# Attention and two MLP layers on one core: second layer in 512-token blocks, float32 scores for three more pairs, q and k in natural order, a new plan

## Chip, core and metric

One Trainium2 chip, one NeuronCore of it. The metric is the device time of one execution in microseconds (us), lower is better. The engines are TensorE (PE: matmuls; PEld: its weight loads), VectorE (DVE), ScalarE (ACT), GpSimd (POOL) and SyncE (SP, which issues most DMAs); SBUF is the on-chip memory, psum the one that matmuls write.

## What is computed

Attention with a threshold, then two MLP layers over the same 2304 = 4 x 576 tokens; everything at float32 accuracy.

```python
def _attn_ref(q, k, v, tau):                       # (4, 8, 576, 64)
    scores = scale * np.matmul(q, k.transpose(0, 1, 3, 2))
    thresh = np.max(scores, axis=-1, keepdims=True) - tau
    scores = np.where(scores >= thresh, scores, -1000000000.0)
    scores = scores - np.max(scores, axis=-1, keepdims=True)
    attn = np.exp(scores)
    attn = attn / (np.sum(attn, axis=-1, keepdims=True) + 1e-09)
    return np.matmul(attn, v)
# x = heads side by side: (2304, 512)
def _moe_ref(x, w_in, w_out):                      # 512 -> 2048 -> 512
    r = np.maximum(x @ w_in, 0.0)
    return (r * r) @ w_out
def _moe2_ref(x, w_in, w_out):
    h = x @ w_in
    sp = np.where(h > 20.0, h, np.log1p(np.exp(np.minimum(h, 20.0))))
    return (h * np.tanh(sp)) @ w_out
```

The four weight matrices come as float64.

## The kernel before

**How the order arises.** The functions of the kernel do not issue instructions. They record operations in a `Plan` (class at line 79): `op({"V": 0.6, "P": 1.24}, fn, r=, w=, x=, due=)` names the engines that may run it (T TensorE, V VectorE, A ScalarE, P GpSimd) with an assumed duration on each, what it reads and writes, and when it is due. `forwards` (line 197) and `backwards` (157) then simulate the engines and choose for each operation an engine and a place, under the assumed durations, the due times and the constants of `PAR` and `BIAS`; it also has a rule for the port that VectorE and GpSimd use together. The program is written out in that order under a manual schedule. So every change of a duration, a due time or a choice can move instructions anywhere.

**Attention.** A pair is two heads of one batch; there are 4 batches of 4 pairs, and a unit is one tile of 128 queries of a pair. `attention` (1005) gives each pair a kind. Kind "d" (batch 0) goes through `job_direct` (678): q and k are loaded in float32 with the two heads as blocks of the free dimension (runs of 1 KB in the memory), and TensorE turns each by 20 small matmuls with the identity; scores are one float32 pass. Kind "s" (batches 1 to 3) goes through `job` (644): q, k, v are loaded in natural order (runs of 256 bytes), scaled by a power of two found from the sums of squares (`pow2`, 551), split into two float16 halves (`split`, 588, lines 600 and 604), turned by DMA, and scores take three float16 passes. In both, `unit` (746) runs the scores, the row maximum (VectorE, line 783, from psum), exp (ScalarE, 806) and the mask with its sum (VectorE, 817, from two SBUF operands). `head` (826) splits the result e into float16 halves (841, and the subtraction at 846 in a piece of 512 and one of 64 columns, on VectorE or GpSimd) where the values are multiplied in float16; batch 0 turns e on TensorE (`values_direct`, 866, line 889).

**Weights.** `weights` (424) fetches one sixteenth of a matrix, [128, 512] float64 as pairs of int32, and rebuilds float32 from the halves by a series of operations on ScalarE (`size`, `rest`), VectorE (`clamp` at 465, `shift` at 477, `sign` at 483; or `factor` on ScalarE and `times`), and to a rounded high part and a low part (`to_hi`, 507; `to_lo`, 519, subtraction at 521). A matmul with weights runs three passes: high-high, high-low, low-high.

```python
            op({"V": 0.34, "P": 1.45}, clamp, x=[w], due=due - 3 + O_CV, two=True)
            op({"V": 0.6}, shift, r=[raw], x=[w], due=due - 2 + O_CV, two=True)
```

**Layers.** Layer one (`first`, 1108, `first_part`, 1116) runs 9 blocks of 256 tokens, each in 8 parts j: two operations of 12 matmuls of 256 columns (`mlp_in`, 1043), ReLU and square, two "down" operations of 12 into the sum `acc`. The first blocks run between units of attention, as soon as batch 0 is done, and the last after it. Layer two (`second`, 1170) runs 9 blocks of 256 tokens in 4 quarters: four `mlp_in` operations into two of three psum places, s0, s1 and the pair (h, o0) (`quarter`, 1028), then softplus and tanh as ScalarE activations (recorded by `act`, 1173, executed at 1179) with steps on VectorE (1223, 1235, gate at 1249), the split into high and low part (511, 521), and four down operations of 6 matmuls of 512 columns:

```python
                for f in range(4):
                    mlp_in(1, 2 * qd + f // 2, f % 2, ph[f // 2], 256 * (f % 2), x, d + 0.1 * f)
```

Of the kernel before, what the change touches and what calls it, by code (L numbers as in the profile page):

```python
# [29 lines left out]
    on=dict(),  # L30
    won=("S", "S"),
    land=1.8,
    lag=1.045,
    turns=("h", "s1"),
    kv=(("nat0", "V1"), ("f1", "nat1"), ("KT1", "f0"), ("V0", "KT0")),
    cd=(-103.359, 8.066, -43.099),
    urg=-3.138,
    rawt=19.607,
    kinds="dddd",
    cgen=0.081,  # L40
    split=(),
    ex=dict(cw=1, cr=22, raw=4, pd=2, sc=4),
    exo=("pd", "cw", "sc", "raw", "cr"),
    blk=list((22.378, 87.527, 172.036, 247.705, 353.772, 474.186, 575.438, 769.06, 852.156)),
    tb2=207.373,
    down2=-110.768,
    sp=(1, 0),
    off=(115.794, 85.638, 120.96, -226.354, 75.139, 25.769, -102.917, -5.246),
    ahead=(13.309, 135.862, 0.835, -119.128, 12.338, 42.57, 40.034, 91.863, 160.78, 84.376),
    start=-49.931,  # L50
    area=dict(sc=("x0", "x1"), hl=("x2",)),
    jobahead=19.218,
    fbi=8,
    stay=-23.036,
    kinds2="ssss",
)
# [22 lines left out]
class Plan:  # L79
# [117 lines left out]
    def forwards(self, succ):  # L197
# [6 lines left out]
        port = 0.0  # L204
# [15 lines left out]
        while count < len(ops):  # L220
# [57 lines left out]
            if o.load is None and (e == "P" or e == "V" and o.two):  # L278
                dur += (0.15 if e == "P" else 0.6) * max(0.0, port - t)
                port = max(port, t + dur)  # L280
# [25 lines left out]
def attention_moe_moe_kernel(ctx: ExitStack, tc: tile.TileContext, q, k, v, tau, w1i, w1o, w2i, w2o, out):  # L306
# [26 lines left out]
    }  # L333
    area = sb.tile([128, 3968], I32, name="area", tag="area")

    def sbuf(place, shape, dt):
        if place in AREA:
            z, n, over = AREA[place]
            n = min(n, math.prod(shape[1:]) * (2 if dt == F16 else 4) // 4)

            def make():
                t = area[:, z:z + n].bitcast(dt)
# [20 lines left out]
    def rot(*places):  # L363
# [7 lines left out]
        "n4": (dict(S=2.95, P=2.75), 1.86, 0.8, 1.9),  # L371
        "q1": (dict(S=0.75, P=0.8), 0.0, 0.4, 0.4), "q2": (dict(S=1.45, P=1.4), 0.62, 0.19, 0.65),
        "w": (dict(S=0.6, P=0.75, A=0.45), 0.0, 1.8, 1.75), "n3": (dict(S=2.3, P=2.0), 1.24, 0.9, 1.6),
        "n2": (dict(S=1.45, P=1.35), 0.62, 0.5, 1.4),
        "xs": (dict(S=0.72, P=0.65), 0.0, 0.36, 0.36), "tail": (dict(S=1.3, P=1.3), 0.6, 0.19, 0.38),
# [46 lines left out]
    W = {}  # L422

    def weights(layer, kind, j, due, places, wplaces):
# [5 lines left out]
        for half in range(2):  # L430
# [15 lines left out]
            def part(t, half=half):  # L446
                if kind == 0:
                    return t()[:, 2 * half:2 * half + 2, :].rearrange("p c f -> p (c f)")
                return t()[:, half, :]
# [929 lines left out]
```

## Time and profile before

| | before |
|---|---|
| time, median of 3 runs | 1058.34 us (1056.44 to 1058.71) |
| the profiled execution | 1057.58 us |
| its span, first to last instruction | 1055.8 us |
| mean granted TensorE clock | 0.987 |
| PE busy | 1012.6 us (96%) |
| DVE busy | 742.9 us (70%) |
| ACT busy | 786.8 us (75%) |
| POOL busy | 119.6 us (11%) |
| first matmul of layer one | 139.8 us after the span's start |
| first matmul of layer two | 685.6 us |
| last matmul | 1050.9 us |

Busy shares are means over stages with different limits, so they are read by stage: attention and weight conversion alone (to 139.8 us), attention with layer one between its units (to about 660), layer two (from 685.6). L392 is the helper `mm` that issues most matmuls; its tile names (acc, h, s, small) say which operation a matmul belongs to.

### The profile page before, as it was taken

The numbers are of one execution on the slowest core, as the hardware profiler recorded it, in microseconds if no ns is written. First come the engines' busy times: TensorE is split into PE (matmuls) and PEld (weight loads), VectorE is DVE, ScalarE is ACT, GpSimd is POOL, SyncE is SP. The second block draws the span as 40 slices with busy tenths as digits, with TensorE's granted clock in tenths as the row PEclk, the third lists the DMA queues.
The fourth block names the chain that finished last, engine by engine and source line by source line (L and its number), as shares of the span: only waits on it lengthen the run. The fifth ranks groups of instructions, "written<-read, shape, count | busy, mean of one in ns | idle before, by whom it ended". The sixth has DMA issues, their size and how long they took to land. (4 is left out here: it accounts for less than half of the span.)

```text
span 1055.8 us, 24074 instructions
## 1 busy us (share of the span) xinstructions
PE 1012.6 (96%) x9484; PEld 915.7 (87%) x9484; DVE 742.9 (70%) x1675; ACT 786.8 (75%) x1301; POOL 119.6 (11%) x132
## 2 busy tenths in 40 slices
PE   6998789799999999999999999899999999999998
PEld 4665478688989898998999999899999999999997
DVE  5999899999888998897574149875454444464443
ACT  5989789787776877776685369978777676596774
POOL 1451333310111111121000000000000000000000
PEclk9999889999999999999999999999999999999999
DMA  9532479889989888976863014410100000000000
GB/s 301 149 125 65 121 160 207 168 155 173 174 153 170 155 185 160 173 156 116 188 212 122 31 37 165 140 55 27 36 14 32 20 21 21 31 30 1 20 21 20
DMA packets 240146, 113.78 MB, mean 108 GB/s; under 512 B 202784, under 2 KB 221728, under 8 KB 240032
## 3 DMA queue, kind: packets, MB, share of 16 engines
q1 hardware_dynamic: 239744, 111.71, 45.9%
q8 instruction: 74, 1.21, 0.5%
q10 hardware_dynamic: 288, 0.52, 0.1%
q14 instruction: 40, 0.33, 0.1%
HBM read 58.33 MB, written 14.16 MB: 69 GB/s over the span
## 5 line engine op out<-in xcount | busy, mean ns | idle before, releaser
L392 PE MATMUL s<-KT,area 64*128 64x64 f16 (+6 forms) x880 | 87.6, 323 | 6.0 <-DVE wi7l L783 1.9
L1175 ACT ACT_TABLE_LOAD x70 | 89.8, 1283 | 1.2
L521 DVE TENSOR_TENSOR gl<-r,gh 128x512 fp32r<-128x512 f32 x83 | 57.0, 687 | 47.1 <-ACT gh L511 45.4
L511 ACT ACTIVATE gh<-r 128x512 fp32r<-128x512 f32 x90 | 56.4, 626 | 31.0 <-PE acc L392 29.0
L806 ACT ACTIVATE e<-area,m 128x576 f32<-128x576 f32 x91 | 68.2, 768 | 15.0 <-DVE hl L846 5.4
L817 DVE SCALAR_TENSOR_TENSOR e<-area,n,e 128x576 f32<-128x576 f32 x91 | 72.6, 814 | 8.0 <-ACT e L806 7.4
L783 DVE TENSOR_SCALAR_CACHE_REDUCE area<-s,c 128x576 f32<-128x576 f32 x91 | 72.1, 812 | 7.3 <-PE s L392 6.7
L1127 ACT ACTIVATE r<-h 128x512 f32<-128x512 f32 x72 | 42.6, 592 | 35.6 <-PE h L392 31.0
L1223 DVE TENSOR_SCALAR area<-area 128x512 f32<-128x512 f32 x37 | 15.7, 426 | 76.0 <-ACT area L1179 75.9
L392 PE MATMUL small<-V,pt 128*128 128x64 f16 (+1 forms) x1680 | 66.4, 196 | 1.7 <-ACT xt L975 0.8
L392 PEld LDWEIGHTS <-pt 128*128 128x128 f16 (+1 forms) x1680 | 56.7, 102 | 10.9 <-issue 7.1
L846 DVE TENSOR_TENSOR hl<-e,hl 128x512 f16<-128x512 f32 (+1 forms) x101 | 61.6, 617 | 4.3 <-ACT hl L841 4.3
L841 ACT ACTIVATE hl<-e 128x576 f16<-128x576 f32 x77 | 51.5, 676 | 13.3 <-DVE e L817 6.0
L846 POOL TENSOR_TENSOR hl<-e,hl 128x64 f16<-128x64 f32 (+1 forms) x53 | 31.0, 587 | 167.5 <-ACT hl L841 158.5
L1179 ACT ACTIVATE area<-area 128x512 f32<-128x512 f32 x74 | 46.1, 630 | 0.5
L1134 ACT ACTIVATE r<-r 128x512 f32<-128x512 f32 x72 | 45.2, 627 | 0.9
L392 PEld LDWEIGHTS <-area 64*128 64x128 f16 (+1 forms) x720 | 23.7, 98 | 24.3 <-issue 3.6
L1179 ACT ACTIVATE area<-s 128x512 f32<-128x512 f32 x24 | 14.3, 596 | 40.2 <-PE s L392 40.0
L521 DVE TENSOR_TENSOR gl<-e,gh 128x512 fp32r<-128x512 f32 x36 | 24.8, 689 | 20.2 <-ACT gh L511 20.1
L470 ACT ACTIVATE area<-area 128x512 int32<-128x512 uint32 x51 | 38.9, 769 | 0.0
L511 ACT ACTIVATE gh<-e 128x512 fp32r<-128x512 f32 x36 | 22.5, 626 | 21.3 <-PE acc L392 21.2
L1249 DVE TENSOR_TENSOR r<-s,area 128x512 f32<-128x512 f32 x23 | 15.9, 691 | 30.4 <-ACT area L1179 30.4
(776 smaller groups left out, 4116.2 us busy)
## 6 DMA issues: line engine op xcount, KB each, us to landing
area<-in_moe_w_in_dram SPq DMA_DIRECT2D x27, 512.0 KB, 4.6
area<-in_moe_w_out_dram SPq DMA_DIRECT2D x24, 512.0 KB, 4.1
xl<-xdr SPq DMA_DIRECT2D x36, 128.0 KB, 2.9
x2dr<-stg SPq DMA_DIRECT2D x18, 256.0 KB, 2.5
xdr<-xs SPq DMA_DIRECT2D x32, 128.0 KB, 2.3
f<-in_v_dram SPq DMA_DIRECT2D x12, 256.0 KB, 3.1
f<-in_k_dram SPq DMA_DIRECT2D x22, 128.0 KB, 3.8
area<-in_q_dram SPq DMA_DIRECT2D x20, 128.0 KB, 2.8
```

The costliest lines, as they stand in the source:

```text
L392: nc.tensor.matmul(o, l, r, start=start, stop=stop, skip_group_check=True)
L511: nc.scalar.activation(out=o, in_=i, func=AF.Copy)
L521: VEC[e].tensor_tensor(out=part(lo), in0=src(), in1=f32(part(hi)), op=ALU.subtract)
L783: nc.vector.tensor_scalar(out=sc(), in0=s()[:, 0:576], scalar1=c()[:, 3:4], scalar2=None, op0=ALU.mult, op1=ALU.min, accum_out=m()[:, i:i ...
L806: lambda e: nc.scalar.activation(out=ex(), in_=sc(), func=AF.Exp, bias=m()[:, i:i + 1], scale=-1.0),
L817: nc.vector.scalar_tensor_tensor(out=ex(), in0=sc(), scalar=nt()[:, i:i + 1], in1=ex(), op0=ALU.is_le, op1=ALU.mult, accum_out=l()[:, 0, u ...
L841: nc.scalar.activation(out=hl()[:, 0:576], in_=ex(), func=AF.Copy)
L846: VEC[e].tensor_tensor(out=hl()[:, a:a + n], in0=ex()[:, z:z + n], in1=hl()[:, z:z + n], op=ALU.subtract)
L1127: nc.scalar.activation(out=halves(r()), in_=turned_out(ph()), func=AF.Relu)
L1134: nc.scalar.activation(out=r(), in_=r(), func=AF.Square)
L1175: nc.scalar.preload_act_table_set({"ln": "natural_log_exp_and_others", "sig": "sigmoid_and_others"}[table])
L1179: nc.scalar.activation(out=out, in_=in_, func=func, **kw)
```

## The change

The second layer takes pairs of blocks: (0,1), (2,3), (4,5), (6,8), and 7 alone. A first-matmul operation then has 512 columns, hidden values of a pair lie in s0 or s1 only, and the second block of a pair sums in h and small. The input is loaded into the place of the low part and split there. In batch 1 the pairs 0, 1 and 3 are of a new kind "h": `job_direct` for q and k, float32 scores, and values as in kind "s". `job_direct` loads natural order with three DMAs and turns with 5 transposes. Scores issue the 64-column piece first. Weights of layer one with j of 3 and more are loaded and converted as one piece of 1024 columns. GpSimd may also run `size` and `rest`, at new assumed costs; layer two uses `factor` and `times` for three of four pieces. 22 transposes of a constant are put on TensorE near the start. SBUF places are regrouped, and the planner has a new model of the shared port and new constants. The core of the diff:

```diff
+    merge=3,
+    warm=(6, 2, 3),
-    blk=list((22.378, 87.527, 172.036, 247.705, 353.772, 474.186, 575.438, 769.06, 852.156)),
+    blk=list((56.005, 116.765, 222.843, 298.566, 412.468, 531.531, 625.519, 840.505, 1014.576)),
-    sp=(1, 0),
+    sp=(0, 3),
+    kb=("hhsh", "ssss", "ssss"),
...
-    BIAS = {"V": 2.329, "A": -28.964, "P": 2.606, "S": 0.46}
+    BIAS = {"V": 1.874, "A": -0.818, "P": 2.37, "S": 0.46}
+    PORT = (0.57, 0.3)
...
+            if o.load is None and e == "P":
+                share = self.PORT[o.two == 2]
+                left_v = port["V"][0] - t
+                if left_v > 0:
+                    dur += 0.15 * min(dur, left_v)
+                    more = min(left_v * share / (1 - share), dur * share)
+                    free["V"] += more
...
-        for half in range(2):
-            raw = sbuf(rot(*places), [128, 512, 2], I32)
-            w = sbuf(rot(*wplaces), [128, 512], F32)
+        for half in range(1 if merged else 2):
+            k = 2 if merged else 1
+            raw = sbuf(rot(*places), [128, 512 * k, 2], I32)
+            w = sbuf(rot(*wplaces), [128, 512 * k], F32)
...
-            op({"V": 0.34, "P": 1.45}, clamp, x=[w], due=due - 3 + O_CV, two=True)
+            op(cost(0.09, A=0.56, P=0.71), size, r=[raw], w=[w], due=due - 4, two=2)
+            op({**cost(0.11, A=0.56, P=0.71), **cost(V=0.34)}, rest, x=[raw], due=due - 3.5 + O_CV, two=2)
+            op(cost(V=0.34, P=0.71), clamp, x=[w], due=due - 3 + O_CV, two=2)
...
+    def warm(stage, before):
+        for _ in range(PAR["warm"][stage]):
+            o = op({"T": 0.25}, lambda e: [
+                nc.tensor.transpose(psum.tile([128, 1024], F32, name="acc", tag="acc")[:, 896:1024], ones, ident)
+                for _ in range(2)
+            ], r=[K], due=1e3)
...
-                e.dma_start(
-                    out=raw()[:, :, j0:main, :].rearrange("p h j d -> p h (j d)"),
...
+                for h in range(2):
+                    e.dma_start(
+                        out=raw()[:, j0:main, h, :],
+                        in_=x[h, 0:512, :].rearrange("(p j) d -> p j d", j=4)[:, j0:main, :],
+                    )
...
-                for j in range(j0, j1):
-                    n = 128 if j < 4 else 64
-                    for h in range(2):
-                        mm(o()[64 * h:64 * h + 64, 128 * j:128 * j + n], raw()[0:n, h, j, :], ident[0:n, 0:n], True, True)
+                    nc.tensor.transpose(
+                        o()[:, 128 * j:128 * j + n], raw()[0:n, j].rearrange("p h d -> p (h d)"), ident[0:n, 0:n]
+                    )
...
-        for i, n in enumerate((*range(NB - 2), NB - 1, NB - 2)):
+        groups = ((0, 1), (2, 3), (4, 5), (6, 8), (7,))
+        for i, ns in enumerate(groups):
...
+            accs = [(acc, [acc[0], acc[0]], (0, 512))]
+            if k == 2:
+                hb, ob = pbuf("h", [128, 512]), plan.buf("o0", lambda: small, over=("o1", "o2"))
+                accs.append(([hb, ob], [hb, ob], (0, 0)))
+            nf = 4 // k
+            for st in range(16 // nf):
+                ph = quarter(k == 1)
+                for f in range(nf):
+                    fc = nf * st + f
+                    mlp_in(1, fc // 2, fc % 2, ph[f * k // 2], 256 * (f % 2) if k == 1 else 0, x, d + 0.1 * f, 256 * k)
```

How this moves instructions is shown at three places. Names are those of the program (s, h, acc, small: psum; a number behind a name tells apart uses of one place; wi, wo: weights with j left in their name before, merged places after).

TensorE in the second layer, at the change from a down operation to the next `mlp_in`, before (x high parts lie in f and e, low parts in f and nat):

```order
L392 MATMUL acc<-wo1h,gh_12518 128x512
L392 MATMUL acc<-wo1h,gl_12522 128x512
L392 MATMUL acc<-wo1l,gh_12518 128x512
L392 MATMUL h<-f_11927,wi4h 128x256
L392 MATMUL h<-f_11938,wi4h 128x256
L392 MATMUL h<-f_11927,wi4l 128x256
```

and in the change, the end of an `mlp_in` and the down operation for the two blocks of a pair:

```order
L428 MATMUL s_11153<-xx,wi_9324 128x512
L428 MATMUL s_11153<-hl,wi_9324 128x512
L428 MATMUL acc<-wo_10264,pt_11145 128x512
L428 MATMUL acc<-wo_10264,pt_11149 128x512
L428 MATMUL acc<-wo_10264,pt_11145 128x512 x2
L428 MATMUL acc<-wo_10264,pt_11149 128x512
L428 MATMUL acc<-wo_10264,pt_11145 128x512
L428 MATMUL h<-wo_10264,pt_11145 128x512
L428 MATMUL h<-wo_10264,pt_11149 128x512
L428 MATMUL h<-wo_10264,pt_11145 128x512
L428 MATMUL small<-wo_10264,pt_11145 128x512
```

The first product now has 512 columns too, and h and small, a place for hidden values before, hold the second block's sum.

GpSimd from its first weight operation on, before (L465 clamp, L521 low part, L492 times):

```order
L465 TENSOR_SCALAR wi7h<-wi7h 128x512
L521 TENSOR_TENSOR wi0l<-stg_136,wi0h 128x512
L465 TENSOR_SCALAR stg_290<-stg_290 128x512
L521 TENSOR_TENSOR wo0l<-stg_222,wo0h 128x512
L492 TENSOR_TENSOR stg_290<-stg_290,wi5l 128x512
L465 TENSOR_SCALAR stg_384<-stg_384 128x512
L521 TENSOR_TENSOR wi1l<-stg_290,wi1h 128x512
L521 TENSOR_TENSOR wi1l<-wi7h,wi1h 128x512
```

and in the change the last weight operations of layer one and what follows them (L525 clamp, L587 low part, L929 the subtraction of e):

```order
L587 TENSOR_TENSOR wo_783<-wo_138,wo_783 128x512
L587 TENSOR_TENSOR wo_1152<-wo_138,wo_1152 128x1024
L525 TENSOR_SCALAR wo_138<-wo_138 128x1024
L929 TENSOR_TENSOR hl<-e,hl 128x64 x2
L525 TENSOR_SCALAR wo_138<-wo_138 128x1024
L929 TENSOR_TENSOR hl<-e,hl 128x64
L587 TENSOR_TENSOR gl_1449<-r,gh_1417 128x512
```

GpSimd's list goes from 137 rows to 55, its weight operations end earlier, and most subtractions of e are on VectorE now.

SyncE's first DMAs, before (L695 and L702 the two parts of a load of q or k, L436 weights):

```order
L695 DMA wi6l<-in_k_dram 128x2x256
L702 DMA wi6l<-in_k_dram 64x2x64
L410 DMA tt<-in_tau_dram 128x1
L436 DMA area<-in_moe_w_in_dram 128x2x512
L695 DMA wo5h<-in_q_dram 128x2x256
L702 DMA wo5h<-in_q_dram 64x2x64
```

and in the change (L776 and L781 the load of q or k, L485 weights):

```order
L485 DMA area<-in_moe_w_in_dram 128x2x512
L776 DMA wo_72<-in_k_dram 128x4x64 x2
L781 DMA wo_72<-in_k_dram 64x2x64
L446 DMA tt<-in_tau_dram 128x1
L776 DMA wo_72<-in_q_dram 128x4x64 x2
L781 DMA wo_72<-in_q_dram 64x2x64
```

The first weight load now stands ahead of k, and a load of q or k is three DMAs.

## Rows read from the trace of the kernel before

**Rows 1.** Whole-stage windows: microseconds and busy times (with instruction counts) by engine.

```profile
...
core 0: us, PE busy (x) PEld busy (x) DVE busy (x) ACT busy (x) POOL busy (x), PEclk, DMA share, GB/s
0.00:139.80 139.80, 114.71 (x993) 79.59 (x993) 119.78 (x297) 112.23 (x218) 46.53 (x40) 0.93 0.50 148
139.80:275.80 136.00, 129.04 (x1537) 115.75 (x1535) 131.90 (x329) 109.61 (x189) 34.51 (x37) 0.99 0.91 176
275.80:619.20 343.40, 340.16 (x3950) 315.53 (x3949) 254.95 (x655) 240.11 (x406) 37.21 (x55) 1.00 0.71 148
619.20:685.60 66.40, 63.49 (x566) 63.11 (x565) 55.79 (x94) 60.80 (x103) 1.34 (x1) 1.00 0.41 136
685.60:1050.90 365.30, 365.23 (x2448) 341.74 (x2448) 180.50 (x304) 262.99 (x384) 0.00 (x0) 1.00 0.07 24
```

**Rows 2.** The chain that ended last: start, length, engine, tile, line.

```profile
...
685.64 4.54 PE h L392 x24
...
950.83 2.68 PE h L392 x24
953.51 5.18 PE acc L392 x24
```

**Rows 3.** Windows as in rows 1, one slice of the second stage.

```profile
...
175.00:200.00 25.00, 22.63 (x263) 20.87 (x261) 25.00 (x57) 21.56 (x37) 8.70 (x7) 1.00 0.86 182
```

**Rows 4.** Timeline of TensorE at the seam: start, length, engine, line, operation, idle before.

```profile
...
685.64 0.46 PE L392 MATMUL h<-f,wi6h 128*128 128x256 f32 x2 [2.50 <-DVE r L1249]
```

**Rows 5.** Groups by line, VectorE, 0 to 276 us: names, shapes, count, busy us, mean ns, idle.

```profile
...
L783 DVE TENSOR_SCALAR_CACHE_REDUCE area<-s,c 128x576 f32<-128x576 f32 x23 | 18.4, 811 | 0.9 <-PE s L392 0.7
...
L817 DVE SCALAR_TENSOR_TENSOR e<-wi7l,n,e 128x576 f32<-128x576 f32 x14 | 12.5, 892 | 0.0
...
L817 DVE SCALAR_TENSOR_TENSOR e<-wi6h,n,e 128x576 f32<-128x576 f32 x12 | 11.9, 989 | 0.0
...
L483 DVE SCALAR_TENSOR_TENSOR stg<-area,stg 128x512 int32<-128x512 int32 x11 | 9.8, 887 | 0.0
...
L465 DVE TENSOR_SCALAR stg<-stg 128x512 f32<-128x512 f32 x15 | 7.9, 524 | 4.7 <-ACT stg L462 4.7
...
L600 DVE SCALAR_TENSOR_TENSOR nat<-f,c,nat 128x640 f16<-128x640 f32 x6 | 5.3, 879 | 0.0
...
L465 DVE TENSOR_SCALAR wi7h<-wi7h 128x512 f32<-128x512 f32 x4 | 1.7, 414 | 0.0
...
L846 DVE TENSOR_TENSOR area<-e,area 128x64 f16<-128x64 f32 x4 | 0.8, 210 | 0.0
...
L483 DVE SCALAR_TENSOR_TENSOR wi7h<-wi4h,wi7h 128x512 int32<-128x512 int32 x1 | 0.7, 690 | 0.0
```

**Rows 6.** Timeline of VectorE and of GpSimd (POOL), about 131 us.

```profile
...
131.62 1.83 DVE L817 SCALAR_TENSOR_TENSOR e<-wo6l,n,e 128x576 f32<-128x576 f32 x1
...
130.36 2.48 POOL L521 TENSOR_TENSOR wo4l<-stg,wo4h 128x512 fp32r<-128x512 f32 x2
...
```

**Rows 7.** Timeline of TensorE, first 14 us.

```profile
...
3.63 2.39 PE L392 MATMUL s<-ident,wi6l 128*64 128x128 f32 x20 [3.63 <-DMA wi6l<-in_k_dram]
...
11.74 2.40 PE L392 MATMUL s<-KT,area 64*128 64x512 f32 x8 [1.61 <-ACT area L718]
```

**Rows 8.** Timeline of TensorE: scores, transposes of e, a turn, float16 scores.

```profile
...
33.06 1.30 PE L392 MATMUL s<-KT,area 64*128 64x512 f32 x8 [0.22 <-DVE wi7l L783]
35.19 0.77 PE L889 MATMUL acc<-ident,e 128*128 128x128 f32 x5 [0.83 <-DVE e L817]
...
36.69 1.36 PE L392 MATMUL s<-ident,wo5h 128*64 128x128 f32 x20
...
148.50 0.93 PE L392 MATMUL s<-KT,area 64*64 64x512 f16 x12 [0.47 <-DVE wi6h L783]
```

**Rows 9.** DMA issues: tile, queue, count, KB each, median us to landing.

```profile
...
f<-in_k_dram SPq DMA_DIRECT2D x22, 128.0 KB, 3.8
...
wi6l<-in_k_dram SPq DMA_DIRECT2D x2, 256.0 KB, 4.7
```

More of the change, by code (lines that the diff above doesn't have):

```diff
@@ L277, in forwards @@
             dur = o.opts[e]
-            if o.load is None and (e == "P" or e == "V" and o.two):
-                dur += (0.15 if e == "P" else 0.6) * max(0.0, port - t)
-                port = max(port, t + dur)
+            if o.load is None and e == "P":
[5 more added lines that the diff above has]
+                    free["V"] += more
+                    port["V"] = (port["V"][0] + more, 0.0)
+                port["P"] = (t + dur, share)
+            elif o.load is None and e == "V" and o.two:
+                left_p, share = port["P"][0] - t, port["P"][1]
+                if left_p > 0:
+                    dur = min(dur / (1 - share), dur + left_p * share)
+                port["V"] = (t + dur, 0.0)
             if e == "A" and o.tab is not None:
@@ L676, in job @@
         job_v(p, due - O_JOB)
+    turns = []
+    def warm(stage, before):
[4 more added lines that the diff above has]
+            ], r=[K], due=1e3)
+            if before is not None:
+                o.deps.add(before.n)
+    warm(0, None)
     def job_direct(p, due):
@@ L891, in values_direct @@
         op({"T": 0.6}, turn, r=[ex, K], w=ts, due=due + 2.5 + O_DIR)
-        more = [z for z in spare["pd"] if z not in plan.last or z in lent]
-        lent.update(more)
+        if p.b == 0:
+            more = [z for z in spare["pd"] if z not in plan.last or z in lent]
+            lent.update(more)
+        else:
+            more = "nat0", "nat1"
         pt = sbuf(rot(*more), [128, 5, 128], F32)
@@ new lines, in second, with lo, __init__, __call__ @@
+            for t in range(k):
+                for xh, xo in zip(hs, os_):
+                    def lo(e, t=t, xh=xh, xo=xo):
+                        VEC[e].tensor_tensor(
+                            out=xo()[:, t], in0=f32(xo()[:, t]), in1=f32(xh()[:, t]), op=ALU.subtract)
+                    op({"V": 0.6, "P": 1.33}, lo, r=[xh], x=[xo], due=d0 - 5, two=1)
+            class Columns:
+                def __init__(self, bufs, k=k):
+                    self.bufs, self.k = bufs, k
+                def __call__(self, c):
+                    return self.bufs[c // 2]()[:, 0:self.k, :, c % 2, :].rearrange("p n a b -> p n b a")
@@ L1304, in layer1 @@
+    def layer1(j):
+        cr = [z for z in spare["cr"] if int(z[2]) > j]
+        cw = [z for z in spare["cw"] if int(z[2]) > j]
+        merged = j >= PAR["merge"]
+        if merged:
+            raws = ["rawA"] + [z[:3] for z in cr if z[3] == "h" and z[:3] + "l" in cr]
+            ws = ["stg"] + cw
+        else:
+            raws = ["raw0", "raw1"] + ["xh", "xo"] * (j < 2) + cr
+            ws = ["stg0", "stg1"] + cw
         d = PAR["cd"][0] + PAR["cd"][1] * j
-        weights(0, 0, j, d, raws, ws)
@@ L1306, in layer1 @@
[L1306 removed]
+        weights(0, 0, j, d, raws, ws, merged)
+        weights(0, 1, j, d + PAR["cd"][2], raws, ws, merged)
     def layer2(j):
[L1309 to L1311 removed]
+        raws = ("raw0", "raw1", "V")
+        again = "KT0 KT1 nat0 nat1".split()
+        once = "f0 f1 e0 e1 hl0 hl1 pt0 pt1 pt2 stg0 r".split()
         order = again + once + 4 * again + ["stg1"]
```

311 lines of the change are left out of this document (173 added, 138 removed).

## The prediction

> **What bounds the kernel now.** I read the busy time of each engine by stage first [rows 1]. Three regions differ. From 275.8 us to 619.2 TensorE works 340.2 of 343.4 us, and in the second layer, from 685.6 to 1050.9, 365.2 of 365.3: there the time is the count of matmuls and nothing else. The chain of work that ended last [rows 2] says the same from behind: through the second layer it is matmuls without a gap, two 256-column operations (24 matmuls) in 2.68 us, 24 of 512 columns in 5.18 us. Up to 275.8 us it is different: TensorE is busy 114.7 of 139.8 and 129.0 of 136.0 us, VectorE 119.8 and 131.9. In finer slices VectorE is full, as in 175 to 200 us with 25.00 of 25, while TensorE works 22.63 [rows 3]. So the first 276 us are set by VectorE, the rest by TensorE. The seam between the layers is a region of its own: TensorE waits there 2.50 us for VectorE's gate [rows 4].
>
> VectorE in the opening is not only full of work, it is slowed. Among its rows up to 276 us [rows 5] the mask (L817, two inputs from SBUF) takes 989 ns in one group of 12 and 892 in another of 14 (four groups hold 52 of them, these are the slowest and the fastest), while the score reduction of the same size (L783, one input, from PSUM) takes 811. The timeline shows why [rows 6]: one mask that starts at 131.62 takes 1.83 us, and GpSimd is at that time in two weight subtractions, from 130.36 for 2.48 us. The mask ends only after GpSimd has ended.
>
> The profiled execution took 1057.58 us, span 1055.8, so 1.8 us lie around the span. It is 0.76 us under the median of the runs shown. The sum below is made against 1057.6.
>
> **The change part by part.**
>
> *Second layer in 512-token blocks.* 8 of the 9 blocks become 4 pairs. Of the 144 first-matmul operations (12 matmuls of 256 columns) 128 become 64 of 12 matmuls of 512 columns; the 864 matmuls of the second product are as before. Two operations of 256 columns took 2.68 us, one of 512 columns takes half of 5.18, 2.59 [rows 2]: 0.09 us saved, 64 times, **−5.8 us**. TensorE bounds this region, so it lies on the path. ScalarE and VectorE have the same elements to do; ScalarE is busy 263.0 of the 365.3 us [rows 1], VectorE 180.5. The pair takes a third psum place (h and small) for its second accumulator, so the hidden values have two places, not three; rival C prices that. Stores per tile replace stores per block, 36 short DMAs over 365 us, with DMA at 7% there [rows 1]: nothing, except at the end, where the last store is as small as now.
>
> *VectorE's work in the opening.* The order of the changed program, counted up to the third block's input (a merged instruction counted as two), has on VectorE: clamps 19 to 22, sign merges 24 to 32, low-part subtractions 23 to 34, multiplications by the sign 4 to 0, splits of q, k, v 14 to 9, 64-column subtractions of e 13 to 30, 512-column ones 34 to 35. With undisturbed durations near the rows [rows 5]: clamps +3 x 0.41 = 1.2 (0.41 in the group of four), signs and subtractions +19 x 0.69 = 13.1, multiplications −4 x 0.69 = −2.8, splits −5 x 0.88 = −4.4, short ones +17 x 0.21 = 3.6, long ones +0.7, the small scale chains of the three pairs about −2. That is +9.4. 37 instructions are merged pairs, which saves a fixed part; a 64-column subtraction takes 0.21 us [rows 5] where an eighth of a 512-column one is 0.09, so a fixed part of about 0.07 (an estimate between 0 and 0.12): −2.6. Sum **+7 us**, on the path.
>
> *GpSimd leaves VectorE alone.* Over the whole program GpSimd goes from 57 long instructions (512 columns or more) to 33, a merged one counted as two, and from 68 short ones to 16. What the contention costs now can be bounded. Below: nothing comes back if VectorE would have waited for something else anyway. Above: 52 masks at some 0.13 above their undisturbed 0.81 are 6.8 us, 11 sign merges at 0.89 against 0.69 are 2.2, 15 clamps at 0.52 against 0.41 are 1.7 [rows 5]; other rows mix shapes, and I estimate as much again, so some 20 us. GpSimd drops about half of its work, so I take **−10 us**, between 0 and −20.
>
> The Trainium skill ("SBUF — State Buffer", section "SBUF: two separate sides") states that VectorE and GpSimd share one port pair as an exclusive lock: a VectorE instruction with two SBUF inputs against a GpSimd one that reads SBUF waits until the other has ended. The single mask of [rows 6] agrees, the means of [rows 5] are far below a full block at each mask. By the rule alone all of GpSimd's 81 us of the opening would cost VectorE something like their length, and half of them returned would be the large gain of rival A.
>
> *The start.* Now the first matmul starts at 3.63 us, when k has landed, and the first turn takes 2.39 us, the first scores 2.40 at 11.74 [rows 7]. The changed order has a weight load ahead of k on SP, three DMAs per load instead of two, and runs of 256 bytes instead of 1 KB. A 128 KB load in such runs lands after 3.8 us in the median, a 256 KB load in 1 KB runs after 4.7 [rows 9], so I expect k about 1 us later. A turn becomes 5 transposes; 5 of that kind take 0.77 us where 20 small matmuls take 1.36 at full clock [rows 8], and at the half clock of the start some 1.2 us less each, twice. Warm-up transposes fill waits. Together **−1 us**, between −4 and +3.
>
> The Trainium skill ("DMA: Bandwidth & Descriptors", section "Specifications") asks for at least 512 bytes a transfer and names a read-modify-write below it, which speaks against the natural order. The two rows do not show such a loss; if it doubled the first two loads the start would be 4 to 5 us later and the sum near 1050.
>
> *Batch 1.* Three pairs take scores from float32: 15 units of 1.30 us instead of 0.93 [rows 8] is +5.5 us of TensorE, six turns of 0.77 are +4.6, and batch 0's eight turns give back 8 x 0.59 = 4.7. Their DMA transposes of q and k go (24 to 18 on SP), which nobody waited for in the rows read. All of this lies before the third block, under VectorE, and costs nothing there; if that cover were gone it would cost **+5 us**. This is late next: if VectorE came out more than 15 us lighter, TensorE would bound the opening.
>
> *The seam.* TensorE loses 2.9 us in its stretch [rows 1], and its first 24 matmuls of layer two take 4.54 us against 2.68 at full clock [rows 2], 1.9 more. The changed order converts the second layer's weights by other due times, and the first pair needs twice the input split before its first matmul (8 short instructions, about 2 us, if nothing hides them). Between −4.8 and +3; I take **−1.5**.
>
> Sum: 1057.6 − 5.8 + 7 − 10 − 1 − 1.5 = 1046.3, predicted **1046 us**.
>
> **Rivals.**
>
> *A: the relief is worth twice as much.* If nearly all of the 20 us and some of TensorE's 32 us of idle time before 275.8 [rows 1] come back, since GpSimd's remaining work lies where VectorE is idle, 15 us more: about 1031. For it: the single mask of [rows 6], and VectorE's full slices. Against: VectorE keeps 7 us more work, and TensorE itself has 5 more. The rule of the first page named above would lead here.
>
> *B: slower, VectorE has GpSimd's work and no relief.* Place: VectorE, from the opening into the blocks after 275.8 us. The 7 us come, the 10 do not, because GpSimd's remaining clamps and subtractions sit on the same masks. And after the third block the order gives VectorE 6 more long and 35 more short subtractions of e (6 x 0.70 + 35 x 0.21 = 11.6 us). It decides if VectorE, at 255 of 343 us there [rows 1], is full in the blocks that still have attention in them. Then 1057.6 − 5.8 + 7 − 1 − 1.5 + 11.6 = 1068. Against it: 26% idle on VectorE in that stretch.
>
> *C: no gain, two places for hidden values stall layer two.* A step has two 512-column operations and four of the second product, 4 x 2.59 = 10.4 us. ScalarE needs 263/36 = 7.3 us per step [rows 1], VectorE's gate 0.7 behind it. The next operation on a place may start 10.4 − 2.6 = 7.8 us after the last one ended. If the chain takes 8.2, 0.4 us are lost in 32 steps: +12, about 1058. Against: ScalarE overlaps the two halves, and half of a step's chain is done well before.
>
> **How the numbers follow.** About 0.2% (2.1 us) is what a measurement of this kernel can tell from no change, so the same is 1056.2 to 1060.5. Forecast 0.62, with its own range 1038 to 1055; A 0.15, B 0.13, C 0.10. Faster: the forecast, A and a little of C, 0.78. Same: most of C, 0.09. Slower: B, 0.13. The range reaches from A's lower end, 1030, to halfway from C towards B, 1062; B at its full price is left out.
>
> **What would show it.** Right: 512-column operations at 2.59 us and the second layer near 359 us between its first matmul and its last; masks (two SBUF inputs) near 0.85 in the opening where they were 0.89 to 0.99; the third block's first matmul near 272 us; GpSimd busy about half of 119.6 us. Wrong: TensorE idle in layer two behind ScalarE or VectorE (C); VectorE at 95% or more past the third block with TensorE waiting for it (B); a third block before 260 us (A); the first scores after 14 us (the loads).

## The result

The changed kernel took 1045.51 us (median of 4 runs, 1043.88 to 1046.22) where the kernel before took 1057.81 (4 runs, 1056.44 to 1058.71). The ratio is 0.9883, with a 95% interval from 0.9866 to 0.9900: 1.2% faster, 12 us. The forecast was 1046. The profiled execution of the changed kernel took 1046.22 us, with a span of 1044.4, 11.4 us less than the 1055.8 of before.

The profile after, its first part (engine, busy us, share, instructions):

```profile
span 1044.4 us, 22116 instructions
...
PE 1016.4 (97%) x8582; PEld 885.0 (85%) x8582; DVE 744.0 (71%) x1693; ACT 796.4 (76%) x1277; POOL 51.7 (5%) x53
```

The windows end at the first matmul of layer one, of its third block and of its ninth block, at 680.1 us, and at the end of the last matmul. They are given with the columns of [rows 1]:

```profile
core 0: us, PE busy (x) PEld busy (x) DVE busy (x) ACT busy (x) POOL busy (x), PEclk, DMA share, GB/s
0.00:131.50 131.50, 112.75 (x834) 69.56 (x834) 110.70 (x265) 99.41 (x181) 19.16 (x23) 0.98 0.53 158
131.50:271.60 140.10, 140.10 (x1587) 122.51 (x1585) 133.53 (x340) 112.28 (x180) 16.57 (x12) 0.99 0.78 157
271.60:611.30 339.70, 338.15 (x3911) 313.87 (x3909) 255.63 (x688) 241.25 (x409) 14.70 (x17) 1.00 0.69 147
...
680.10:1039.60 359.50, 357.05 (x1735) 313.63 (x1734) 194.55 (x324) 278.75 (x403) 1.27 (x1) 1.00 0.09 30
```

Against [rows 1]: the third block's first matmul is at 271.6 instead of 275.8 us (−4.2), the ninth block's at 611.3 instead of 619.2 (another −3.7), the last matmul ends at 1039.6 instead of 1050.9 (another −3.4). The forecast had −4 for the first stretch and −7.3 for the two others together, which came to −7.1. The border between these two is not comparable by itself, since the new order puts other work ahead of the ninth block.

The fourth border needs a correction. The first matmul of layer two is not at 685.6 us in the kernel before, as its table says: that matmul opens the last quarter of layer two's first block (weights wi6h). The first one stands earlier, between matmuls of layer one; here it is in the kernel before and in the changed one:

```profile
655.42 0.39 PE L392 MATMUL small<-f,wi1h 128*128 128x256 f32 x2
...
640.83 0.38 PE L428 MATMUL s<-f,wi 128*128 128x512 f32 x1
```

From there to the end of the last matmul it is 395.5 us before and 398.8 in the change, with matmuls of layer one in between in both. So the sign of the prediction, "near 359 us between its first matmul and its last", can't be read off as it stands; the 359.5 us of the last window start inside layer two's first pair. What layer two gained shows in its steps.

One thing in these rows was not forecast: in the second stage TensorE is busy 140.10 of 140.10 us. In [rows 1] it was 129.04 of 136.00, and VectorE was the full engine. In the changed kernel TensorE is the bound from the first matmul of layer one on. In the last window it has one long wait, for VectorE:

```profile
683.61 0.46 PE L428 MATMUL s<-f,wi 128*128 128x512 f32 x1 [2.02 <-DVE stg L1363]
```

A step of layer two is as forecast. The chain of the changed kernel (start, length, engine, tile) shows two 512-column operations in 5.18 us, a new pair of them every 10.36:

```profile
953.37 5.18 PE s L428 x24
963.73 5.18 PE s L428 x24
```

In its first microseconds the changed kernel has something that the forecast had taken lightly, here the timeline of TensorE (start, length, line, operation, matmuls, idle before):

```profile
5.68 1.39 PE L790 MATMUL s<-ident,wo 128*128 128x128 f32 x5 [5.68 <-DMA wo<-in_k_dram]
8.00 1.39 PE L790 MATMUL s<-ident,wo 128*128 128x128 f32 x5 [0.93 <-DMA wo<-in_q_dram]
9.31 4.21 PE L750 MATMUL acc<-ident,ones 128*128 128x128 f32 x8
13.46 2.51 PE L428 MATMUL s<-KT,area 64*128 64x64 f32 x8
15.89 7.41 PE L750 MATMUL acc<-ident,ones 128*128 128x128 f32 x14
23.23 2.51 PE L428 MATMUL s<-KT,area 64*128 64x64 f32 x8
```

A row of scores bears the shape of its first matmuls, four of 64 columns; four of 512 are in its eight too. k lands at 5.68 instead of 3.63 us [rows 7], the turns take 1.39 instead of 2.39, and then the 22 warm-up transposes of line 750 take 4.21 and 7.41 us. The first scores start at 13.46, later than the 11.74 of before.

### The profile page after: what moved, and what is told of

It reads as the page before. It is cut to its first block, busy times and chain, and to the rows that moved or that the text cites. A ratio compares the mean times of both kernels' runs of the same rounds, so it can differ in the third digit from the quotient of the medians.

```text
span 1044.4 us, 22116 instructions
## 1 busy us (share of the span) xinstructions
PE 1016.4 (97%) x8582; PEld 885.0 (85%) x8582; DVE 744.0 (71%) x1693; ACT 796.4 (76%) x1277; POOL 51.7 (5%) x53
## 4 chain that ended last, share of the span: by engine, by line
PE 80%; ACT 10%; DVE 5%; issue 3%; DMA 1%; SPq 0%; DVEq 0%; ACTq 0%
PE acc L428 25%; PE h L428 21%; PE s L428 20%; PE small L428 10%; ACT area L1266 2%; DVE e L900 1%; ACT L1262 1%; PE acc L750 1%; PE s L790 1%; ACT area L530 1%; PE s L1169 1%; ACT gh L576 1%; DVE area L866 1%; ACT area L554 1%; ACT e L889 1%
## 5 line engine op out<-in xcount | busy, mean ns | idle before, releaser
L428 PE MATMUL h<-xh,wi 128*128 128x256 f32 x1152 | 218.5, 282 | 0.4 <-ACT r L1214 0.4
L428 PE MATMUL acc<-gh,wo 128*128 128x256 f32 x1152 | 215.7, 280 | 0.0
L428 PEld LDWEIGHTS h<-xh,wi 128*128 128x128 f32 x1152 | 184.4, 193 | 10.3 <-issue 4.7
L428 PEld LDWEIGHTS acc<-gh,wo 128*128 128x128 f32 x1152 | 183.1, 192 | 5.5 <-issue 4.7
L428 PE MATMUL h<-xo,wi 128*128 128x256 f32 x576 | 159.0, 276 | 0.0
L428 PE MATMUL acc<-gl,wo 128*128 128x256 f32 x576 | 158.5, 275 | 0.0
L428 PEld LDWEIGHTS h<-xo,wi 128*128 128x128 f32 x576 | 111.1, 193 | 0.0
L428 PEld LDWEIGHTS acc<-gl,wo 128*128 128x128 f32 x576 | 110.6, 192 | 0.0
L428 PE MATMUL s<-KT,area 64*128 64x512 f16 (+7 forms) x820 | 95.6, 358 | 4.0 <-DVE xo L1186 2.3
L587 DVE TENSOR_TENSOR gl<-r,gh 128x512 fp32r<-128x512 f32 x80 | 55.3, 691 | 51.5 <-ACT gh L576 49.8
L428 PE MATMUL acc<-wo,gh 128*128 128x512 f32 x240 | 79.8, 380 | 0.0
L929 DVE TENSOR_TENSOR hl<-e,hl 128x512 f16<-128x512 f32 (+1 forms) x137 | 67.5, 499 | 1.4 <-ACT hl L924 1.1
```

What stands on the lines that cost most here:

```text
L428: nc.tensor.matmul(o, l, r, start=start, stop=stop, skip_group_check=True)
L587: VEC[e].tensor_tensor(out=part(lo), in0=src(), in1=f32(part(hi)), op=ALU.subtract)
L929: VEC[e].tensor_tensor(out=hl()[:, a:a + n], in0=ex()[:, z:z + n], in1=hl()[:, z:z + n], op=ALU.subtract)
```

## The experiments

Where an edit says that the order is kept, the plan is made as in the kernel it starts from, and only what the operations issue, or the engine that issues them, is changed. Where it says planned again, the planner ran on the edited program. A ratio is to the kernel before, measured beside the run (1056.5 to 1057.6 us); a difference between two runs is one of medians.

**1. The 512 columns alone.** Order kept.

```diff
-                    mm(ph()[:, col:col + n], l()[:, c, 128 * f:128 * f + 128], r(c),
-                       c == 0 and i == 0, c == 3 and i == 2)
+            for t in range(2 if n == 512 else 0):
+                for c in range(4):
+                    for i, (l, r) in enumerate(passes(wi, x)):
+                        mm(ph()[:, 256 * t:256 * t + 256], l()[:, c, 128 * f:128 * f + 128], r(c)[:, t],
+                           c == 0 and i == 0, c == 3 and i == 2)
```

> The changed kernel with its order kept, but each 512-column matmul of the first product in layer two written as two of 256 columns. Theory: layer two is bound by TensorE, so 64 operations cost 0.09 us more each: +5.8 us, about 1051.3 where the changed kernel has 1045.5; the time to the first matmul of layer two stays. Rival: ScalarE or VectorE set layer two in the changed kernel, and the wide matmuls gave nothing: less than +2 us.

Measured 1050.44 us, ratio to before 0.9928 (0.9909 to 0.9947): 4.9 us slower than the changed kernel. The chain of waits of this kernel:

```profile
943.73 5.36 PE s L428 x48
954.27 5.36 PE s L428 x48
```

A step takes 10.54 us instead of 10.36. With 0.18 us for each of 32 steps that is the 5.8 of the forecast; the 4.9 agree with it. In the profiled executions layer two, from its first matmul to its last, is 3.7 us longer (402.5 against 398.8), and it starts 2.2 us earlier, which the edit does not explain. Layer two is bound by TensorE, and the wide matmuls are worth about what their rows said.

**2. Without the warm-up transposes.** Order kept.

```diff
-            o.fn(o.eng)
+            if "warm" not in o.fn.__qualname__:
+                o.fn(o.eng)
```

> The changed kernel with its order kept, without the 22 warm-up transposes. Theory: they fill waits; the first scores come a little earlier (about 12 us instead of 13.5) or at a lower clock; within 1.5 us of 1045.5. Rival: they hold up the clock of the first units and so carry a part of the gain of the opening: 3 us or more slower without them.

Measured 1038.57 us, ratio 0.9820 (0.9799 to 0.9841): **7 us faster** than the changed kernel (0.9883, 0.9866 to 0.9900; the intervals do not meet). Both guesses failed, the second with the wrong sign. The timeline of TensorE without the transposes:

```profile
10.23 2.50 PE L428 MATMUL s<-KT,area 64*128 64x64 f32 x8 [1.08 <-ACT area L801]
13.65 3.23 PE L428 MATMUL s<-KT,area 64*128 64x64 f32 x8 [0.91 <-DVE wo L866]
...
20.46 2.51 PE L428 MATMUL s<-KT,area 64*128 64x64 f32 x8
...
25.03 1.65 PE L790 MATMUL s<-ident,wi 128*128 128x128 f32 x10
...
27.96 1.35 PE L428 MATMUL s<-KT,area 64*128 64x64 f32 x8
```

The second scores start at 13.65 (they take 3.23 us as their second head starts 0.73 us after the first) where they had waited until 23.23 behind 14 transposes on TensorE's own queue. What follows was late by nearly as much: the first scores at 1.35 us start at 27.96 here and at 36.76 in the changed kernel.

```profile
36.76 1.35 PE L428 MATMUL s<-KT,area 64*128 64x64 f32 x8
```

The third block's first matmul is at 262.5 here, 9.1 us earlier than in the changed kernel: next to nothing of the delay had been made up. Nor do the transposes bring the clock forward. Scores of this kind take 2.5 us at the lower of TensorE's two levels (1.2 GHz) and 1.35 at the upper (2.4 GHz). With the transposes the scores at 23.23 still take 2.51, although TensorE's rows show no gap from 9.31 on (its weight loads did stand still, see run 3). The column of the granted clock reads 1.00 in all of this stretch and doesn't show the difference.

The first two stages of this kernel, with TensorE 11 us less busy in the first than in the changed kernel:

```profile
0.00:120.90 120.90, 101.33 (x812) 65.12 (x812) 109.05 (x264) 98.71 (x181) 19.12 (x23) 1.00 0.59 171
120.90:262.50 141.60, 139.88 (x1586) 122.16 (x1584) 134.45 (x341) 113.21 (x181) 15.70 (x13) 0.99 0.76 156
```

This version beats both kernels. It is the base of five of the runs below.

**3. Why a warm-up transpose is slow.** Order kept, two destinations instead of one.

```diff
-                nc.tensor.transpose(psum.tile([128, 1024], F32, name="acc", tag="acc")[:, 896:1024], ones, ident)
-                for _ in range(2)
+                nc.tensor.transpose(
+                    psum.tile([128, 1024], F32, name="acc", tag="acc")[:, 768 + 128 * z:896 + 128 * z], ones, ident)
+                for z in range(2)
```

> The changed kernel with its order kept and its 22 warm-up transposes, but each pair of them writes two places of psum in turn, not the same one. Without them the kernel took 1038.6 us, with them 1045.5; one took 0.53 us where a transpose of e at the same clock took about 0.25. Theory: they are slow because each writes where the one before wrote; with two places they take about half, and some 4 of the 7 us come back: 1041 to 1042. Rival: the operand of ones or the kind of transpose makes them slow: no change, 1045.5.

Measured 1045.72 us, ratio 0.9899 (0.9879 to 0.9919), and 14 transposes still take 7.41 us. Two places did not help, and the traces show why one takes 0.53 us where five transposes of e at the same level take 1.27. These are the weight loads (PEld), first a warm-up transpose of the changed kernel, then one of this run, then the five of e in the changed kernel:

```profile
9.85 0.18 PEld L750 LDWEIGHTS acc<-ident,ones 128*128 128x128 f32 x1 [0.35 <-PE acc L750]
...
9.32 0.18 PEld L750 LDWEIGHTS acc<-ident,ones 128*128 128x128 f32 x1 [0.35 <-PE acc L750]
...
28.30 1.08 PEld L972 LDWEIGHTS acc<-ident,e 128*128 128x128 f32 x5
```

The weight load of a warm-up transpose waits 0.35 us for the transpose before it to end, 20 times in 22; the loads of e follow each other without a wait. The wait is as long with two places, so this run did not take away what makes them slow. Neither the constant nor writing one place is slow in itself: in run 12 five transposes of the same constant into the same columns take 0.77 us, as five of e do in [rows 8].

```profile
103.90 0.77 PE L760 MATMUL s<-ident,ones 128*128 128x128 f32 x5
```

In the program the two differ in that a warm-up transpose calls `psum.tile` anew each time, where run 12 writes a tile that is there. That this call makes the wait is likely, and no run tries it alone.

**4. The loads and turns of before.** Order of run 2 kept, 1 KB runs, two DMAs, 20 small matmuls.

```diff
-                for h in range(2):
-                    e.dma_start(
-                        out=raw()[:, j0:main, h, :],
...
+                e.dma_start(
+                    out=z[:, :, j0:main, :].rearrange("p h j d -> p h (j d)"),
...
-                    nc.tensor.transpose(
-                        o()[:, 128 * j:128 * j + n], raw()[0:n, j].rearrange("p h d -> p (h d)"), ident[0:n, 0:n]
-                    )
+                    for h in range(2):
+                        mm(o()[64 * h:64 * h + 64, 128 * j:128 * j + n], z[0:n, h, j, :], ident[0:n, 0:n], True, True)
```

> The changed kernel with its order kept, without warm-up transposes, and with the loads and turns of q and k of the kernel before (1 KB runs, two DMAs, 20 small matmuls) in all seven pairs of float32 scores. Theory: VectorE sets the opening, 14 turns at 0.59 us more hide under it, the first turns cost 2 us more and the loads land 1 us earlier: 1039 to 1042 (1038.6 without the edit). Rival: TensorE, busy 28.8 of 30 us in parts of the opening, is bound as well there: 14 x 0.59 = 8 us, about 1047.

Measured 1046.58 us, ratio 0.9912 (0.9889 to 0.9935): 8.0 us slower than run 2, the rival's value. The stages:

```profile
0.00:125.60 125.60, 107.62 (x963) 70.98 (x963) 110.00 (x265) 100.06 (x181) 19.53 (x23) 0.99 0.53 165
125.60:268.80 143.20, 141.43 (x1646) 123.58 (x1644) 134.13 (x340) 113.07 (x180) 14.65 (x12) 1.00 0.78 153
```

4.7 us are lost before layer one's first matmul, where ten of the 14 turns lie, and 1.6 more up to the third block. TensorE's busy time grows by 6.3 and 1.6 us in the two stages, with VectorE's nearly unchanged. So most of the matmuls' time of a turn is on the path in the opening, also where VectorE looks full. This edit exchanges the loads too. k lands for the first turn at 5.56 us in run 2 and at 5.49 here, behind the same weight load:

```profile
5.56 1.38 PE L790 MATMUL s<-ident,wo 128*128 128x128 f32 x5 [5.56 <-DMA wo<-in_k_dram]
...
5.49 4.70 PE L428 MATMUL s<-ident,wo 128*64 128x128 f32 x40 [5.49 <-DMA wo<-in_k_dram]
```

The shorter runs cost nothing at the start. That k comes 2 us later than in the kernel before goes with what stands ahead of it in the queue.

**5 and 6. GpSimd empty, before and after.** Order kept in both, all of GpSimd's arithmetic on VectorE.

```diff
-            o.fn(o.eng)
+            e = o.eng
+            if e == "P" and "V" in o.opts:
+                e = "V"
+            o.fn(e)
```

Of the kernel before:

> The kernel before with its order kept, all of GpSimd's arithmetic on VectorE. In the opening VectorE gets 13 clamps (5.3), 24 low parts (16.6), 4 products (2.8), 2 long and 23 short subtractions (6.2): 31 us; GpSimd's 81 us go. With the 0.25 us of contention per us of GpSimd work that the prediction used: -20, so +11, about 1069. With the 0.41 that the run of the changed kernel without GpSimd gave ((16 - 1.5)/35.7): -33, so about 1056. Rival A (full block): 1030 or less. Rival B (no relief): 1088.

Measured 1058.20 us, ratio 1.0015 (0.9998 to 1.0032): no difference. Its groups on VectorE (names, count, busy, mean ns) answer to [rows 5]:

```profile
L817 DVE SCALAR_TENSOR_TENSOR e<-wi7l,n,e 128x576 f32<-128x576 f32 x14 | 11.4, 815 | 0.0
...
L817 DVE SCALAR_TENSOR_TENSOR e<-wi6h,n,e 128x576 f32<-128x576 f32 x12 | 9.8, 814 | 0.0
```

and its first two stages to [rows 1]:

```profile
0.00:139.50 139.50, 116.27 (x991) 80.77 (x992) 122.37 (x326) 113.46 (x218) 0.85 (x7) 0.93 0.51 148
139.50:278.20 138.70, 130.33 (x1539) 117.08 (x1536) 132.96 (x368) 110.54 (x189) 0.00 (x0) 0.98 0.87 171
```

The masks are back at 0.81 us. By the count of the expectation VectorE took over 31 us of work, and it is busy 255.3 us up to the third block where it was 251.7: some 27 us of its busy time before was standing still beside GpSimd, about 0.34 us for each of GpSimd's 81. It is neither the 0.25 of the prediction nor a full block. In the kernel before, GpSimd's work gained nothing.

Of the changed kernel:

> The changed kernel with its order kept, all of GpSimd's arithmetic on VectorE. In the opening VectorE gets clamps 4.1, low parts 6.2, low parts of activations 4.1, short subtractions 1.5, 16 us in all; GpSimd's 35.7 us go. Theory (0.25 us of contention for each us of GpSimd): -9, so +7 us, 1050 to 1054, and the masks all near 0.81. Rival A (full block): -30 and more of contention, so faster by 10 us. Rival B (no relief): +16.

Measured 1046.47 us, ratio 0.9898 (0.9877 to 0.9918), 1 us more than the changed kernel and within its interval. One group of masks in the changed kernel and then here:

```profile
L900 DVE SCALAR_TENSOR_TENSOR e<-wi,n,e 128x576 f32<-128x576 f32 x34 | 29.9, 886 | 0.1
```

```profile
L900 DVE SCALAR_TENSOR_TENSOR e<-wi,n,e 128x576 f32<-128x576 f32 x34 | 27.4, 812 | 0.3 <-ACT e L889 0.2
```

By the same kind of count 16 us of work came to VectorE and about 14 us of standing still went (0.4 per us of GpSimd's 35.7), and what was left did not move the end.

**7. The short subtractions back on GpSimd.** Order of the changed kernel kept.

```diff
+            if e == "V" and o.opts == {"V": 0.14, "P": 0.3}:
+                e = "P"
```

> The changed kernel with its order kept, but every 64-column subtraction of e on GpSimd (about as the kernel before had most of them). Theory: VectorE loses 32 of them in the opening, 32 x 0.21 = 6.7 us at least, and pays contention at about 20 us per 81 us of GpSimd work, 32 x 0.55 x 0.25 = 4.4: about -2 us, 1043 to 1046. Rival A (each GpSimd instruction blocks a mask for nearly its whole length): 32 x 0.55 = 18 us less 6.7: +8 us or more. Rival B (no contention cost): -6.7.

Measured 1044.55 us, ratio 0.9877 (0.9854 to 0.9901), not distinguishable from the changed kernel. GpSimd works 18 us more up to the third block, VectorE 4 us less, and TensorE is again full in the second stage:

```profile
130.90:270.50 139.60, 139.60 (x1580) 122.03 (x1579) 129.59 (x306) 112.00 (x180) 34.26 (x44) 0.99 0.75 157
```

The rate of runs 5 and 6 does not hold for these short instructions. A 64-column subtraction takes VectorE 0.22 us when GpSimd is empty (run 6), so 32 of them are 7.0 us, of which 4 came out: GpSimd's 18 us more cost VectorE some 3, about 0.17 us for each (an estimate), and the group of masks shown for run 6 stays at 884 ns.

Runs 5 to 7 say the same of the time: who does this work, VectorE or GpSimd, makes no difference that can be measured.

**8. Merged weight operations taken apart.** Order of run 2 kept. Each operation of a merged piece is issued in two halves (`each` calls it for columns 0 to 511 and 512 to 1023).

```diff
-            op(cost(0.06, V=0.6), shift, r=[raw], x=[w], due=due - 2 + O_CV, two=1)
+            op(cost(0.06, V=0.6), each(shift), r=[raw], x=[full], due=due - 2 + O_CV, two=1)
```

> The changed kernel with its order kept, without warm-up transposes, and with each 1024-column weight operation of the ten merged pieces written as two of 512 on its engine (loads stay merged). The prediction put the saving of merging at 2.6 us of VectorE, on the path. Theory now: VectorE and TensorE take turns as the bound in the opening, so 0 to +3 us over 1038.6. Rival: merging carries a large part of the gain of the opening, also through ScalarE: +5 or more.

Measured 1042.32 us, ratio 0.9862 (0.9832 to 0.9892), against 0.9820 for run 2: 3.7 us slower, of which 2.2 show in the span of the profile (1038.5 against 1036.3). The intervals of the two ratios overlap, so the price is not sure. The 2.6 of the prediction fits it, but not as VectorE's alone: VectorE is busy 1.3 us longer up to the third block, ScalarE 2.1 and GpSimd 3.3, whose instructions the edit divides too.

**9. The plan alone.** Run 2, planned again.

```diff
-    fbi=7,
+    fbi=8,
```

> The changed kernel without warm-up transposes, planned again with eight refinements instead of seven, and nothing else. It measures what planning again does by itself. Theory: the plan carries little, within 3 us of 1038.6, and the 23 us of the run with four float16 pairs are their price. Rival: planning again alone moves the time by 10 us or more, and that run can't be read as a price.

Measured 1049.14 us, ratio 0.9929 (0.9902 to 0.9956): 10.6 us slower with the same operations. The rival holds. The constants of a plan fit one plan, and 11 us, nearly as much as the whole change, hang on it.

**10 and 11. Fewer float32 pairs.** Run 2 with `kb=("ssss", ...)`, and with `kb=("hhss", ...)`, both planned again.

> The changed kernel without warm-up transposes and with all four pairs of batch 1 in float16 halves (kind s), planned again. Theory (VectorE sets the opening up to the third block): six splits of 0.88, the scale chains and the sums of squares come back to VectorE, +7, and TensorE's 10 us less give nothing: about 1045. Rival (TensorE is bound there): 1030 to 1036.

Measured 1061.47 us, ratio 1.0042 (1.0025 to 1.0059), 23 us slower than run 2, slower than before even.

> The changed kernel without warm-up transposes, with two pairs of batch 1 in float32 scores instead of three, planned again. Theory: each float32 pair is worth a third of the 23 us: about 1046. Rival: the constants fit one plan only; then about as slow as with four float16 pairs, or as far off as the plan made with eight refinements.

Measured 1045.75 us, ratio 0.9896 (0.9866 to 0.9925), 7 us slower than run 2. After run 9 neither is a price: 7 us lie within what a new plan moves, the 23 do not, but their part is unknown. The windows of the run with four float16 pairs show where it is slow:

```profile
90.00:120.00 30.00, 23.34 (x166) 15.85 (x166) 24.92 (x59) 23.35 (x37) 1.04 (x1) 0.66 0.51 133
120.00:150.00 30.00, 20.28 (x175) 16.73 (x170) 29.90 (x63) 22.38 (x38) 5.04 (x5) 0.78 0.52 128
```

TensorE is busy 43.6 of 60 us there and its granted clock has fallen to 0.66 and 0.78. That suggests that the float32 scores, longer work for TensorE between batch 0 and layer one, keep the clock up. Run 12 tries this.

**12. Filling TensorE's waits in the kernel before.** Order kept.

```diff
         def scores(e):
+            more(e)
+            for _ in range(fill[0]):
+                nc.tensor.transpose(ss[0]()[:, 896:1024], ones, ident)
```

> The kernel before with its order kept, and five transposes of a constant behind the scores of each of the last seven units ahead of layer one (35 in all, into unused columns of the scores' psum place). The kernel before shows a granted clock of 0.71 from 100 to 116 us and 0.74 from 132 to 148, where TensorE had waited for VectorE. Theory: the fall of the clock costs some 6 to 8 us there; the transposes take about 9 us, mostly in waits, and keep the clock near 1: -2 to -6 us, about 1053. Rival: the clock falls all the same or TensorE is the bound: +5 us or more.

Measured 1058.65 us, ratio 1.0027 (1.0007 to 1.0047). The windows with it, the two stretches that the expectation names:

```profile
100.00:116.00 16.00, 14.25 (x99) 9.21 (x99) 14.21 (x36) 13.55 (x28) 4.58 (x3) 0.90 0.59 161
...
132.00:148.00 16.00, 12.79 (x146) 10.73 (x147) 16.00 (x41) 11.92 (x22) 5.05 (x7) 0.73 0.61 157
```

The clock rose in one stretch, 0.71 to 0.90, and not in the other, and the time did not fall. Keeping TensorE busy with nothing is no gain here. Whether the float32 pairs help by the clock stays open.

## Why the prediction was right, and where it was not

The predicted 1046 and the measured 1045.5 agree, and so do the regions: the opening ended 4.2 us earlier (4 forecast), the rest came 7.1 us shorter (7.3). By its terms:

- *Second layer, −5.8.* Right, and shown alone by run 1 (4.9, and 0.18 us per step in the chain). Rival C fell: TensorE idles 2.4 us in the stretch from 680.1 us, 2.0 of them in one wait for VectorE at 683.61; a stall of 0.4 us per step, as that rival has it, would be 12.
- *VectorE's work +7 and relief −10.* The direction of the net is right: VectorE is busy 244.2 us up to the third block instead of 251.7. The relief was taken too small. Run 5 gives 0.34 us of VectorE's time for a us of GpSimd's, run 6 about 0.4, so by these rates the drop from 81 to 36 us returned 15 to 18 (an estimate). "From 0 to −20" held it. But the sum took VectorE's time as time of the kernel, and no run shows that: runs 5 to 7 moved VectorE's busy time by 3.6, 1.8 and −4.0 us, and the end by less than these measurements can tell (the interval of run 5 reaches to +3.4 us). The single-mask row [rows 6] had suggested a full block and the means [rows 5] a small cost; the means were nearer.
- *The start, −1.* Wrong, the step "Warm-up transposes fill waits". They stand on TensorE's queue ahead of the second scores, and run 2 puts their cost at 7 us, mostly in the 9.6 us by which those scores came late. The order of TensorE's instructions would have shown it: 8 transposes stand ahead of the first scores and 14 between the first and the second. No duration was given to them in the sum, and the plan assumed 0.25 us for two (in the diff) where they take 1.07. The rest of this term was about right: without the transposes the first scores start at 10.23 us where they had started at 11.74, since a turn takes 1.0 us less (1.2 forecast) and k comes about 2 us later (1 forecast).
- *Batch 1, the turns.* Wrong too, that all of this lies "under VectorE, and costs nothing there". Run 4 shows that 14 turns of 20 matmuls instead of 5 transposes cost 8.0 us. The kernel before has eight of them, in batch 0; by count their share is some 4.6 us (an estimate), where the sum had 2.4, for the first two. The other six are new, and by the same run what batch 1 adds to TensorE should be on the path too, at least in part; no run prices it. In the second stage the reason is that TensorE was the bound (140.10 of 140.10), with VectorE lighter. The text had set that point at 15 us less work on VectorE; the 7.5 us of the line above were enough. Over the first stage as a whole neither engine is full (in run 2 TensorE 101.33 and VectorE 109.05 of 120.90 us), and why the turns cost so much there stays open.
- *The seam, −1.5.* Taken too large. The wait is still there, 2.02 us where [rows 4] had 2.50, and the twelve matmuls behind it take 4.4 us where 2.6 is usual, 1.8 more (1.9 in the kernel before). So about 0.5 came back here. It is no seam between the layers either, but a wait inside layer two's first block or pair, for the gate on VectorE that frees a place for hidden values: rival C's stall, once and not in every step. The sum over the two stretches fits all the same.

So the errors of the opening cancelled. The warm-up cost 9.1 us up to the third block, and without it the rest of the opening gave 13.3 us where 4 had been forecast. Batch 0's turns are about 2 of these 9 us, and the others are not assigned to a cause. The sum was right to half a microsecond by chance; that it would be faster, and that layer two gives 5 to 6 us, were not. About half of the 15 us by which rival A goes beyond the forecast was within reach: without the warm-up the kernel takes 1038.6. Rival B did not happen: VectorE is busy 255.6 of 339.7 us past the third block, as before.

What stays open is how the gain of the opening without warm-up, 13.3 us up to the third block (262.5 against 275.8), divides. Taken back one by one, the new turns are 6.3 of it (run 4) and merging 2.5 (third block at 265.0 in run 8); the other 4.5 belong to the float32 pairs, the change of engines and the plan together, and run 9 shows why new plans can't separate them. The granted clock goes with them: in the first stage it is 0.93 in the kernel before, 0.98 in the changed one and 1.00 without the warm-up. How much of the gain that carries, no run separates.

## What to carry to other kernels

A filler that is meant for idle time still stands in its engine's queue: count its duration against the start of what comes behind it, look in the trace whether its instructions wait for each other, and run the kernel once without it. Two engines that both look nearly full take turns as the bound, so lighter work on one is worth only the distance to the other, and work added to the second is not free. Where a planner sets the order, test a part with the order kept; a new plan alone moved this kernel by 11 us.

## What the runs showed of the hardware that was not expected

- 22 transposes of a constant, 128x128 float32, took 0.53 us each (14 in 7.41 us), about twice a transpose of e at the same level of the clock (5 in 1.27 us): each weight load waited 0.35 us for the transpose before it. Without that wait the same constant took 0.77 us for 5 in run 12. From 9.31 to 23 us TensorE did such transposes and one operation of scores, and the scores at 23.23 still ran at the lower level (2.51 us).
- GpSimd's work beside VectorE cost VectorE 0.34 to 0.4 us for each us that GpSimd was busy, and about 0.17 where it was 64-column subtractions alone (run 7). The Trainium skill's rule ("SBUF — State Buffer", section "SBUF: two separate sides") of an exclusive lock fits the single mask of [rows 6] (1.83 us). Over a stage the cost was a third to two fifths of what a full block of VectorE for all of GpSimd's time would be.
- The Trainium skill's limit of 512 bytes for a transfer at full rate ("DMA: Bandwidth & Descriptors", section "Specifications") did not show in the loads of q and k: k landed for the first turn at 5.56 us in 256-byte runs (run 2) and at 5.49 in 1 KB runs (run 4).
